# Products of values over the last 64 keys: from 64x64 pieces of the array to 128 rows padded with zeros

## The chip, the cores and the metric

The kernel runs on one core of a Trainium2 chip. A core has TensorE (PE in the profile, with its weight loads shown apart as PEld), VectorE (DVE), ScalarE (ACT), GpSimd (POOL) and SyncE (SP), which here only issues DMAs. The metric is the device time of one launch in microseconds (us); lower is better. Before the change the median of four runs is 1345.78 us (1345.26 to 1347.38).

## The reference, cut to what matters

Attention with a hard threshold is followed by a two-layer MLP with a squared ReLU. All of it is in fp32.

```
batch, n_heads, seq, head_dim = (8, 8, 576, 64)
scores = scale * np.matmul(q, k.transpose(0, 1, 3, 2))
thresh = np.max(scores, axis=-1, keepdims=True) - tau
scores = np.where(scores >= thresh, scores, -1000000000.0)
attn = np.exp(scores - np.max(scores, axis=-1, keepdims=True))
attn = attn / (np.sum(attn, axis=-1, keepdims=True) + 1e-09)
attn_out = np.matmul(attn, v)                 # the products of values
x = attn_out.transpose(0, 2, 1, 3).reshape(B * S, H * D)   # 4608 x 512
h = x @ w_in                                  # 512 x 2048
out = (np.maximum(h, 0.0) ** 2) @ w_out       # 2048 x 512
```

## The kernel before, in words

**Tiling.** Two heads of one batch make a pair, u = 0 and 1, and a pair is one visit `n`; there are 36 visits. The 576 queries and the 576 keys are each four blocks of 128 and a rest of 64. A step handles one block of 128 queries for both heads: `scores` or `scores_of_two` (TensorE), `maxima` (VectorE, L305), `exponents` (ScalarE, L317 to L320), `threshold` (VectorE, L332 to L335), `divide` (GpSimd, L340 and L342).

**Transposed weights.** The products of values contract over keys, so keys must lie on the partitions. `wT` holds the transposed attention weights: 128 partitions, ten groups of 64 queries, and nine columns of keys. Columns 0 to 3 are the four key blocks of head 0, columns 5 to 8 those of head 1, and column 4 (`NBLK`) is shared: the 64 last keys of one head lie on partitions 0 to 63 and those of the other on partitions 64 to 127. In the first 11 visits `turn` fills `wT` with TensorE transposes (L381, L388, L394) and ScalarE copies (L382, L390, L395). From visit 11 on (`by_dma`) `turn_blocks` transposes 32x32 blocks on VectorE into `turned` (L425 to L435), `set_aside` writes these to DRAM (`aside`, L403), and `place_blocks` brings them to their partitions by DMA (L443 and, for the rest of 64 queries, L452 and L460). All of these DMAs are issued in program order by SP.

**Products of values.** `mix(n, cols)` is the subject (L493 to L526). The stationary operand is a tile of values `vs`, keys by 64 columns, and the moving one is `wT`. Head 0 writes partitions 0 to 63 of a PSUM bank and head 1 partitions 64 to 127, so its matmuls use half the columns of the array each: "128\*64" in the profile. The last 64 keys have only 64 rows: "64\*64". In the first 11 visits `mix` runs once for every block of queries, 35 times in all: eight 128\*64 matmuls and two 64\*64 ones over 128 queries (over 64 for the rest block). Those calls are named early below. From visit 11 on it runs once a visit, 25 times, named late: group ONE is 320 queries (the region ONE or ODD of `wT` and the rest region LEFT), group TWO is 256 queries. It issues sixteen 128\*64 matmuls for both groups first and then four 64\*64 ones. For these, group ONE takes its heads' keys from (above, below) and group TWO from (below, above), so that the four products use four different quarters of the array. To make this possible `turn_blocks` swaps the two heads' rest keys for query blocks 2 and 3 (`i < 2` is the plain case): two narrow transposes instead of one. Each fp32 matmul shows as two records in the trace, a pair of heads as four.

**Values.** `load_v` loads `vs` (two buffers): the four key blocks of each head, and the last 64 keys of both heads into both halves of the partitions, since a head's keys are needed above for one group and below for the other.

**Order.** Each engine's instructions stand in the order in which the Python program records them; only semaphores tie engines together. A planner in the kernel spreads TensorE pieces of the MLP (`mlp_in` L544; `unit` L655; `mlp_out` L726; `product` L761) between the attention's steps, by constants of its own (`PIECE_US`, `VALUES_US`) that do not know the durations of `mix`. `put` copies `mix`'s results from PSUM to `xT` with ScalarE (L479, L483, L490). The functions that the change touches, and what calls them:

## Time and profile before

| | before |
|---|---|
| median of 4 runs | 1345.78 us |
| the profiled execution's own time | 1345.56 us |
| its span, first to last instruction | 1343.8 us |
| mean granted TensorE clock | 0.994 |
| busy: PE / DVE / POOL / ACT | 97% / 69% / 57% / 43% |
| `mix` (L496), PE busy | 169.9 us in 1700 records |
| ... of it 64\*64 records over 320, 256, 128 queries | 19.5, 16.7, 12.2 us |
| narrow transposes L429 and L430 (DVE) | 50 each, 202 and 204 ns |
| one transpose of both (L427, DVE) | 50, 270 ns |

The span is what the trace covers; the execution's own time has 1.8 us more around it. "Busy" counts the time in which at least one instruction of an engine runs, so that matmuls which run side by side in different parts of the array share it. An idle gap carries the name of what ended it: "[0.83 <-DVE w L332]" means 0.83 us idle until VectorE's instruction of line 332 had written `w`. A timeline row that merges several records shows the start of the first.

### The profile page before, as it was taken

What the parts mean: (1) busy time and instruction counts of PE and PEld (TensorE: products, weight loads), DVE (VectorE), ACT (ScalarE), POOL (GpSimd) and SP (SyncE); (2) the same over time, 40 slices, a digit from 0 to 9 for tenths busy, and PEclk for the clock granted to TensorE, in tenths of its full rate; (3) what the DMA queues carried; (4) which work ended last, traced back from release to release, by engine and by line L of the source; (5) the groups of instructions that cost most, each with busy time, mean ns of one, the idle gap of its engine ahead of it and who ended that gap; (6) DMA issues with size and microseconds to landing.
All of it is one profiled execution on the core that took longest, in us unless ns stands there. A gap on an engine that the chain in (4) does not pass through costs nothing.

```text
span 1343.8 us, 25020 instructions
## 1 busy us (share of the span) xinstructions
PE 1301.4 (97%) x9112; PEld 1078.8 (80%) x9112; DVE 924.9 (69%) x2026; ACT 581.7 (43%) x1357; POOL 761.5 (57%) x861
## 2 busy tenths in 40 slices
PE   6899999989999999999999999999999999999998
PEld 5676556878787878778897988888897888889997
DVE  6877775868687777777777776869687877632231
ACT  4777674225253434435353534343435353522421
POOL 3679775754654646474647463737374737354451
PEclk7999999999999999999999999999999999999999
DMA  7764531737696767766686766758686766430000
GB/s 155 164 160 113 145 91 35 163 84 189 147 215 137 191 163 172 167 154 159 147 201 156 179 175 133 177 137 192 139 199 156 177 166 149 136 92 1 17 17 16
DMA packets 331883, 187.04 MB, mean 139 GB/s; under 512 B 293200, under 2 KB 293232, under 8 KB 325360
## 3 DMA queue, kind: packets, MB, share of 16 engines
q1 hardware_dynamic: 326656, 176.22, 56.2%
q0 software_dynamic: 2800, 8.93, 1.9%
q8 instruction: 72, 1.18, 0.4%
q10 hardware_dynamic: 2304, 0.29, 0.2%
q14 instruction: 51, 0.42, 0.1%
HBM read 109.58 MB, written 68.42 MB: 132 GB/s over the span
## 4 chain that ended last, share of the span: by engine, by line
PE 84%; DVE 4%; ACT 4%; DMA 3%; SPq 1%; POOL 1%; issue 1%; DVEq 0%; POOLq 0%
PE big L761 28%; PE big L655 27%; PE big L496 11%; PE big L284 8%; PE big L544 3%; PE big L268 3%; PE big L726 2%; PE big L381 2%; DMA aside<-turned 1%; DVE w L332 1%; ACT w L320 1%; DVE st L305 1%; ACT wT L382 1%; DMA wT<-aside 1%; SPq L452 1%
## 5 line engine op out<-in xcount | busy, mean ns | idle before, releaser
L305 DVE TENSOR_REDUCE st<-big 128x1 f32<-128x576 f32 x288 | 204.7, 750 | 136.7 <-PE big L284 102.7
L342 POOL TENSOR_SCALAR w<-w,st 128x576 f32<-128x576 f32 x269 | 255.3, 958 | 27.8 <-DVE st L335 23.4
L340 POOL TENSOR_SCALAR st<-st 128x2 f32<-128x2 f32 (+1 forms) x148 | 35.6, 241 | 369.6 <-DVE w L332 364.9
L761 PE MATMUL big<-wo,gsum 128*128 128x256 f32 x1088 | 245.0, 382 | 0.0
L761 PEld LDWEIGHTS big<-wo,gsum 128*128 128x128 f32 x1088 | 204.3, 190 | 38.6 <-issue 11.7
L332 DVE SCALAR_TENSOR_TENSOR w<-big,st,w 128x576 f32<-128x576 f32 x269 | 206.9, 805 | 36.6 <-ACT w L320 36.1
L761 PE MATMUL big<-wo,g 128*128 128x256 f32 x816 | 186.4, 382 | 0.0
L655 PE MATMUL big<-xT,w_in_sb 128*128 128x128 f32 x1536 | 185.6, 276 | 0.0
L320 ACT ACTIVATE w<-big,st 128x576 f32<-128x576 f32 x269 | 183.5, 733 | 0.0
L655 PEld LDWEIGHTS big<-xT,w_in_sb 128*128 128x128 f32 x1536 | 179.0, 192 | 3.8 <-issue 3.1
L496 PE MATMUL big<-wT,vs 128*64 128x128 f32 (+7 forms) x1700 | 169.9, 358 | 11.5 <-ACT wT L382 4.0
L761 PEld LDWEIGHTS big<-wo,g 128*128 128x128 f32 x816 | 151.2, 190 | 26.3 <-issue 7.2
L496 PEld LDWEIGHTS big<-wT,vs 128*64 128x64 f32 (+1 forms) x1700 | 97.3, 137 | 80.3 <-issue 25.5
L317 ACT ACTIVATE st<-st 128x2 f32<-128x2 f32 (+1 forms) x148 | 30.1, 204 | 256.3 <-DVE st L305 255.5
L667 DVE TENSOR_TENSOR g<-big,g 128x512 f32<-128x512 f32 x96 | 65.2, 681 | 87.7 <-PE big L655 83.5
L284 PE MATMUL big<-kT,qT 64*128 64x256 f32 (+3 forms) x768 | 108.8, 416 | 4.8 <-ACT seen L297 2.7
L284 PEld LDWEIGHTS big<-kT,qT 64*128 64x128 f32 x768 | 85.1, 186 | 21.3 <-issue 5.6
L425 DVE STREAM_TRANSPOSE turned<-w 128x512 f32<-128x512 f32 x100 | 70.3, 703 | 25.6 <-DMA aside<-turned 22.8
L534 POOL TENSOR_TENSOR gsum<-g 128x512 f32<-128x512 f32 x34 | 45.1, 1326 | 74.0 <-ACT g L664 71.9
L663 ACT ACTIVATE g<-g 128x512 f32<-128x512 f32 x96 | 60.2, 627 | 57.4 <-DVE g L667 57.3
L664 ACT ACTIVATE g<-g 128x512 f32<-128x512 f32 x128 | 80.7, 630 | 4.1
L431 DVE STREAM_TRANSPOSE turned<-w 128x512 f32<-128x512 f32 x100 | 66.9, 669 | 0.0
(112 smaller groups left out, 1960.5 us busy)
## 6 DMA issues: line engine op xcount, KB each, us to landing
aside<-turned SPq DMA_DIRECT2D x50, 1152.0 KB, 4.5
wT<-aside SPq DMA_DIRECT2D x200, 288.0 KB, 5.3
vs<-in_v_dram SPq DMA_DIRECT2D x72, 128.0 KB, 5.6
ql<-in_q_dram SPq DMA_DIRECT2D x126, 72.0 KB, 4.5
wo<-in_moe_w_in_dram SPq DMA_DIRECT2D x16, 512.0 KB, 4.6
wo<-in_moe_w_out_dram SPq DMA_DIRECT2D x16, 512.0 KB, 3.6
out_dram<-osb POOLq DMA_DIRECT2D x32, 256.0 KB, 3.4
kl<-in_k_dram SPq DMA_DIRECT2D x113, 72.0 KB, 3.0
```

Source lines behind the costliest of these rows:

```text
L284: nc.tensor.matmul(big[to, at + x0:at + x1], lhsT, keys[u * D:(u + 1) * D, x0:x1], start=True, stop=True)
L305: nc.vector.tensor_reduce(out=mx[:, u:u + 1], in_=sc[u], axis=AX.XY, op=ALU.max)
L320: nc.scalar.activation(out=w[:, u, :].rearrange("p (h k) -> p h k", h=2), in_=sc[u], func=AF.Exp, bias=bias[:, u:u + 1], scale=SCALE)
L332: nc.vector.scalar_tensor_tensor(out=wu, in0=sc[u], scalar=thr[:, u:u + 1], in1=wu, op0=ALU.is_ge, op1=ALU.mult, accum_out=sm[:, u:u + 1])
L342: nc.gpsimd.tensor_scalar(out=w[:, u, :], in0=w[:, u, :], scalar1=z[:, u:u + 1], scalar2=rcp[:, u:u + 1], op0=ALU.add, op1=ALU.mult)
L425: move(wb[:, 0:h, :, :], whole_[:, 0, :, :, :])
L431: move(wb[:, h + 1:, :, :], whole_[:, 1, :, :, :])
L496: nc.tensor.matmul(ps[u * D:(u + 1) * D, :], vs[n % 2][rows, u * (NBLK + 1) + c, :], wT[rows, at // REST:(at + ps.shape[1]) // REST, NBLK ...
L655: nc.tensor.matmul(to[:, f, :], factor(j, p, q, c)[:, f * P:(f + 1) * P], part[:, c, :], start=(p in "125" and f == 0 and c == 0), stop=(p ...
L664: nc.scalar.activation(out=to, in_=to, func=AF.Square)
L667: nc.vector.tensor_tensor(out=x, in0=to, in1=x, op=ALU.add)
L761: nc.tensor.matmul(to, left[:, f, :], wo[:, slot, f, :], start=(f == 0), stop=(f == HF - 1))
```

## The change

The last 64 keys' values of head u now lie in rows `u * 64` to `u * 64 + 63` alone, and the other 64 rows of that tile are set to zero once, at the start, in both buffers (four memsets of 64x64 on GpSimd). Column 4 of `wT` keeps both heads' keys; a head's product now runs over all 128 rows, and the other head's weights meet zeros. All ten matmuls of a group are 128\*64, and a group's last keys follow its other blocks directly: first all of ONE, then all of TWO. The swap for query blocks 2 and 3 goes, and with it the split of one transpose in two. The values' last keys are loaded once, not twice: before visit 12 four DMAs a visit instead of six, later four of half the size for two of them.

```diff
+    def last_keys(t, u, filled=True):
+        half = u if filled else 1 - u
+        return t[half * D:(half + 1) * D, u * (NBLK + 1) + NBLK, :]
 def load_v(n):                                  # paired visits
-            for half in range(2):
-                loads.append((both[half * D:(half + 1) * D, :, NBLK, :], src[:, NBLK * P:S, :].rearrange("u p d -> p u d")))
+                loads.append((last_keys(t, u), src[u, NBLK * P:S, :]))
 ...                                             # the others
-            for half in range(2):
-                todo.append((t[half * D:(half + 1) * D, at + NBLK, :], v[b, h + u, NBLK * P:S, :]))
+            todo.append((last_keys(t, u), v[b, h + u, NBLK * P:S, :]))
 def turn_blocks(vis, i):
-            if i < 2:
-                move(wb[:, h, :, :].rearrange("p (u j) q -> p u j q", u=2), rest_[:, :, 0, :, :])
-            else:
-                move(wb[:, h, 2:4, :], rest_[:, 0, 0, :, :])
-                move(wb[:, h, 0:2, :], rest_[:, 1, 0, :, :])
+            move(wb[:, h, :, :].rearrange("p (u j) q -> p u j q", u=2), rest_[:, :, 0, :, :])
 def mix(n, cols):
-        groups = (one[:, 0:n1], at, (above, below)), (two[:, 0:n2], TWO, (below, above))
-        for ps, x, _ in groups:
-            for c in range(NBLK):
-                for u in range(2):
-                    term(ps, u, c, x, first=(c == 0))
-        for ps, x, places in groups:
-            for u, rows in enumerate(places):
-                term(ps, u, NBLK, x, rows, last=True)
+        def terms(ps, at):
+            for c in range(NBLK + 1):
+                for u in range(2):
+                    nc.tensor.matmul(ps[u * D:(u + 1) * D, :], vs[n % 2][:, u * (NBLK + 1) + c, :],
+                                     wT[:, at // REST:(at + ps.shape[1]) // REST, NBLK if c == NBLK else u * (NBLK + 1) + c, :],
+                                     start=(c == 0), stop=(c == NBLK))
+        terms(one[:, 0:2 * P + REST], at)
+        terms(two[:, 0:2 * P], TWO)
 ...                                             # at the start
+    for t in vs:
+        for u in range(2):
+            nc.gpsimd.memset(last_keys(t, u, False), 0.0)
```

## The prediction

> **What bounds the kernel now.** I read the page first, then the PE's busy time by stretch, then its idle gaps, and last the matmuls of `mix` one by one.

> ```profile
> PE 1301.4 (97%) x9112; PEld 1078.8 (80%) x9112; DVE 924.9 (69%) x2026; ACT 581.7 (43%) x1357; POOL 761.5 (57%) x861
> PE 84%; DVE 4%; ACT 4%; DMA 3%; SPq 1%; POOL 1%; issue 1%; DVEq 0%; POOLq 0%
> ```

> PE is busy for 97% and makes 84% of the chain of waits. Of the 42 us that PE is idle, almost all lies before 584 us; after that the waits view shows one gap of 0.3 us, and the last 3.5 us are the final stores. So late matmul time counts in full, and before 584 us I must look at each place.

> Now one late `mix`. Each row is the PE (or weight load) timeline asked at an instant, so its start is that of the oldest record still running.

> ```profile
> 809.04 0.75 PE L496 MATMUL big<-wT,vs 128*64 128x320 f32 x3
> 809.36 0.14 PEld L496 LDWEIGHTS big<-wT,vs 128*64 128x64 f32 x1
> 810.70 0.44 PE L496 MATMUL big<-wT,vs 128*64 128x320 f32 x2
> 812.32 0.60 PE L496 MATMUL big<-wT,vs 128*64 128x256 f32 x4
> 812.75 0.80 PE L496 MATMUL big<-wT,vs 128*64 128x256 f32 x6
> 813.07 0.76 PE L496 MATMUL big<-wT,vs 64*64 64x320 f32 x8
> 813.75 0.38 PE L655 MATMUL big<-held,w_in_sb 128*128 128x128 f32 x1
> ```

> Records of the two heads start together: the halves run side by side. The first pair of records takes 0.32 (809.04 to 809.36); the next take (810.70 - 809.36) / 5 = 0.268 over 320 queries, and (812.75 - 812.32) / 2 = 0.215 over 256. The last should end its slot at 812.97, but the first 64\*64 starts at 813.07: 0.10 for the change of shape. Then eight 64\*64 records, four at a time, hold PE until 813.75 (a slot of 0.32, one of 0.27, and 0.10 for the change back). Whole: 4.71 us.

> An early `mix` of 128 queries:

> ```profile
> 85.96 0.33 PE L496 MATMUL big<-wT,vs 128*64 128x128 f32 x2
> 86.78 0.54 PE L496 MATMUL big<-wT,vs 128*64 128x128 f32 x4
> 86.99 0.44 PE L496 MATMUL big<-wT,vs 64*64 64x128 f32 x4
> 87.35 0.33 PE L381 MATMUL big<-ident,w 128*128 128x128 f32 x1
> ```

> Eight pairs of records, the last at 86.78; a slot is 0.11, so 86.99 again holds 0.10 of change; the two 64\*64 products, which use two quarters only, take 86.99 to 87.35. Whole: 1.39 us.

> **Late: the four quarters go.** After, ONE and TWO have ten pairs of records each: 0.32 + 9 x 0.268 + 10 x 0.215 + 0.10 for leaving the shape = 4.98 against 4.71: +0.27 us a late `mix`. The 0.10 for 128\*64 to 128\*128 has no row; the same two shapes in the other direction (808.83 to 809.04 for a slot of 0.11), 128\*64 to 64\*64 and 64\*64 to 128\*128 all show 0.09 to 0.10, so I take 0.10. Its ends: nothing, or twice that. A row stands for each other term.

> [...]

> There are 25 late calls. Twenty-one lie where PE is continuous or on the chain that ends the gap behind them: 21 x 0.27 = +5.7. Four differ.

> *The call at 504.65.* The gap after it is ended by another chain (the stores and SP's DMAs since 493, which do not hold this `mix`):

> ```profile
> 528.76 1.51 PE L284 MATMUL big<-kT,qT 64*128 64x256 f32 x10 [0.83 <-DVE w L332]
> ```

> 0.83 swallows 0.27: I count 0 (ends 0 and +0.27).

> *The call at 277.9.* It is the first one, and what follows waits on SP:

> ```profile
> 283.10 11.27 SPq L452 DMA_DIRECT2D wT<-turned  x16
> 300.35 0.71 DVE L425 STREAM_TRANSPOSE turned<-w 128x512 f32<-128x512 f32 x1 [3.20 <-DMA aside<-turned]
> 303.41 2.20 PE L284 MATMUL big<-kT,qT 64*128 64x256 f32 x14 [0.51 <-DVE w L332]
> 306.85 0.70 PE L284 MATMUL big<-kT,qT 64*128 64x256 f32 x2 [1.23 <-ACT seen L297]
> ```

> SP has nothing to do from 280.65 to 283.10: its L452 overwrite the region LEFT, which in the old order is read last by the 64\*64 products at `mix`'s very end (283.07). In the new program these DMAs wait for ONE's last matmul, which ends before TWO's ten slots: 283.07 + 0.27 - 0.10 - 10 x 0.215 = 281.1, some 1.9 us earlier. Behind them on SP stand three loads and the store to `aside`, for whose landing VectorE waits 3.20 us; then come `threshold` and PE, with gaps of 0.51 and 1.23. ScalarE's exponents (done at 298.8) leave room. Up to 1.74 goes; the sum L667 of VectorE, which wants PE's L655 first, is late next and holds some of the 1.23. I take 1.3 off and 0.27 on: -1.0. Ends: +0.27 (nothing of it arrives) and -1.5. In the other visits the same early release only lets SP wait for a VectorE store later (L403), so no gain is counted.

> *The calls at 428.9 and 574.0.* Here PE waits inside `mix` for the DMA that brings TWO (gaps of 0.25 and 2.68). The new order puts two slots of 320 queries, 0.54, before that wait and takes 8 x 0.215 + 0.10 + 0.68 = 2.50 to 2.25, 0.25 less, after it. At 428.9 the gap of 0.25 goes and the end stays: 0. At 574.0:

> ```profile
> 276.19:279.60 3.41, 1.70 (x12) 1.46 (x14) 3.34 (x11) 0.00 (x0) 0.68 (x2) 1.00 0.85 136
> 576.56:579.97 3.41, 0.91 (x9) 0.77 (x11) 3.09 (x6) 1.66 (x4) 3.41 (x5) 1.00 1.05 133
> 579.97:583.38 3.41, 3.41 (x19) 1.44 (x16) 1.20 (x6) 0.15 (x1) 2.94 (x5) 0.50 0.36 55
> ```

> PE was busy for 0.91 of 3.41 us, and in the next 3.41 us the granted clock (the column after POOL) is 0.50; a stretch with 1.70 busy of 3.41 was followed by no such drop. After, the gap shrinks to 2.68 - 0.54 = 2.14, so at least 1.27 of 3.41 is busy: between the two rows, and either is possible. At half clock the remainder took 4.09; without it ten slots of 0.215 and 0.10 are 2.25. Ends: -0.3 (still slow) and -1.9; I take -1.0.

> [...]

> **Early: a change of shape goes.** With two products there were only two quarters in use, so a pair of heads over 128 rows costs the same slots. After: 0.82 + 2 x 0.11 + 0.21 = 1.25 against 1.39, -0.14 a call (a call over 64 queries comes out the same from its rows). Where `turn`'s L394 follows, itself 64\*64, the change of shape only moves: 7 calls at 0. Seven others lie in the first loop, where PE waits for VectorE 0.55 us a step and the chain passes them by, as it does five more between 98 and 209 us, where GpSimd's rounding or ScalarE holds it:

> ```profile
> 40.78 0.49 PE big L381 x3
> 41.30 0.86 ACT wT L382 x2
> ```

> Followed through all 35 calls, the chain of waits holds 16 whose saving counts: 16 x 0.14 = -2.2. Ends: -0.8 (other engines are close behind and take up two thirds) and -2.6.

> **The rest.** VectorE: 404 ns of two transposes become 270, 50 times; start to start it is 0.25 against 0.20, and only three pairs stand on the chain (at 301, 418 and 565 us): -0.15. Elsewhere PE's 97% hide it. The four memsets: POOL's next work after its start-up is at 15.49, after 11.4 us idle, and a 128x128 memset takes 0.22: nothing (with the cover gone at most 0.9). Values: 24 DMAs less on SP, at a median 0.53 each, in a stretch where SP is not on the chain: nothing, or -0.3. `put` of ONE runs under TWO now; ScalarE is not late behind `mix`: nothing. No wait is added.

> **Sum.** 5.7 + 0 - 1.0 + 0 - 1.0 - 2.2 - 0.15 = +1.3 us on the profiled 1345.56, which is 0.2 under the median of the runs. So 1347.1 for the median, with the price of leaving the shape, 37 times 0.10 either way, the widest of the unknowns.

> **Rivals.**
> - *Only the loss is real* (slower). The early saving is taken up by waits (-0.8), SP's early start does not reach PE (+0.27), the clock falls at 580 us again (-0.3), and 504.65 counts: 5.7 + 0.27 + 0.27 - 0.3 - 0.8 - 0.15 = +5.0, 1350.8. For it: ScalarE and VectorE end many early gaps of 0.24 to 1.4 us. Against it: between 66 and 90 and between 158 and 206 us the chain is nearly all PE. It counts as slower from +2.7, that is if 1.4 of the 4.3 us taken off above is missing. Chance 0.32.
> - *Leaving 128\*64 for 128\*128 is free* (faster). Then each of the 37 calls on the chain loses 0.10, and the slow first slot behind it (0.10 where 128-column weights follow): 1.3 - 37 x 0.2 = -6.1, 1339.7. It decides from 0.11 a call. Against it: every other change of shape, in the reverse direction too, shows 0.09 to 0.10. Chance 0.05.
> - *More waits shrink than I see* (faster): ScalarE and SP are released 2.2 us earlier in all 25 late calls, and the 9 us of gaps between 298 and 530 could lose 4 more: 1343. Against it: those gaps end on VectorE or ScalarE work that starts from scores. Chance 0.04.

> **How the numbers follow.** The forecast, gains and losses nearly cancelling, has 0.59. A measurement of this kernel can tell about 0.2%, 2.7 us, from no change: 1343.1 to 1348.5. The forecast's own range is 1345 to 1349.5, and some 0.09 of its 0.59 lies above 1348.5; of the first rival's 0.32 some 0.06, where half of the savings come, lies below. So same 0.59 - 0.09 + 0.06 + 0.01 of the third = 0.57, slower 0.35, faster 0.08. The range reaches to the first rival: 1344.0 to 1350.9.

> **What would show it.** No 64\*64 L496 rows; a late `mix` of 4.98 and an early one of 1.25 between the starts of its neighbours; SP's L452 near 281.3 in place of 283.1 and smaller gaps at 303 to 307; a gap of some 2.1 us inside the call near 574, with the clock behind it at 0.5 or 1. Wrong if the next matmul after `mix` starts directly at its slot's end, if early gaps grow by what `mix` saves, or if the clock falls at other places.

## The result and the profile after

The changed kernel takes 1348.12 us (median of 43 runs), the kernel before 1345.86 us (64 runs). The ratio is 1.0017 with a 95% interval of 1.0012 to 1.0022: 2.3 us slower, where 1.3 was forecast, and inside 0.2%. The profiled execution took 1347.66 us, its span is 1345.9 us.

The page after: busy time of the engines, and the chain of waits by engine.

```profile
PE 1304.4 (97%) x9112; PEld 1088.9 (81%) x9112; DVE 924.1 (69%) x1976; ACT 583.2 (43%) x1357; POOL 761.4 (57%) x865
PE 83%; DVE 5%; ACT 4%; DMA 3%; SPq 2%; POOL 1%; issue 1%; DVEq 0%; POOLq 0%
```

PE is busy 3.0 us longer and the bound is the same. Next, one late call of `mix` and one early call, PE asked at instants as before; `mix` is L497 now.

```profile
808.12 0.49 PE L497 MATMUL big<-wT,vs 128*64 128x320 f32 x2
812.59 0.60 PE L497 MATMUL big<-wT,vs 128*64 128x256 f32 x4
812.81 0.39 PE L497 MATMUL big<-wT,vs 128*64 128x256 f32 x2
813.12 0.38 PE L643 MATMUL big<-held,w_in_sb 128*128 128x128 f32 x1
```

```profile
85.66 0.33 PE L497 MATMUL big<-wT,vs 128*64 128x128 f32 x2
86.69 0.28 PE L497 MATMUL big<-wT,vs 128*64 128x128 f32 x2
86.90 0.33 PE L384 MATMUL big<-ident,w 128*128 128x128 f32 x1
```

The late call takes 813.12 - 808.12 = 5.00 us where it took 4.71; the early one 1.24 where it took 1.39. Leaving the shape costs what was assumed: 813.12 - 812.81 is a slot of 0.215 and 0.10.

The place near 277 us, now 2 us earlier: SP's stores of the rest region and PE's gaps behind them.

```profile
275.94 7.15 PE L497 MATMUL big<-wT,vs 128*64 128x320 f32 x40 [2.57 <-DVE w L335]
280.96 11.53 SPq L451 DMA_DIRECT2D wT<-turned  x16
298.46 0.71 DVE L428 STREAM_TRANSPOSE turned<-w 128x512 f32<-128x512 f32 x1 [0.91 <-DMA aside<-turned]
302.52 2.20 PE L287 MATMUL big<-kT,qT 64*128 64x256 f32 x14
305.32 0.70 PE L287 MATMUL big<-kT,qT 64*128 64x256 f32 x2 [0.60 <-ACT seen L300]
```

The call ends at 283.0, but SP starts at 280.96, with ONE's end: two of PE's gaps, 0.51 and 1.23 before, are 0 and 0.60. The call itself took 7.15 us, not 5.2. The windows view tells why (the clock is the column after POOL):

```profile
273.06:276.47 3.41, 0.84 (x5) 0.34 (x5) 2.80 (x6) 0.00 (x0) 0.00 (x0) 1.00 0.71 114
276.47:279.88 3.41, 3.41 (x15) 2.93 (x15) 3.34 (x9) 0.31 (x3) 2.66 (x3) 0.50 0.44 69
575.05:578.46 3.41, 1.92 (x16) 0.73 (x12) 3.41 (x8) 0.82 (x3) 3.41 (x4) 1.00 1.22 181
578.46:581.87 3.41, 3.27 (x24) 2.48 (x25) 2.44 (x7) 1.58 (x5) 2.94 (x4) 1.00 0.44 60
```

In this execution the clock fell to a half at 276.5 us and not near 580; in the profiled execution before it was the other way round. So the two profiles each carry one such window, at different places. And the gap inside the call near 574:

```profile
578.60 2.38 PE L497 MATMUL big<-wT,vs 128*64 128x256 f32 x20 [1.63 <-DMA wT<-aside]
```

Comparing the starts of the same call in the two traces (after minus before) gives the course: -0.14 us at the first call, -1.44 at the last early one (236.7), -1.97 at 277.9, -1.53 at 331.3, -0.67 at 428.9, -0.86 at 480.5, -0.58 at 504.6, -0.23 at 553.3, +0.05 at 574.0, -2.11 at 631.0, and then about +0.28 a call to +1.79 at the last one; PE's end is +2.07.

Two traces can be compared only so far. A second trace of the kernel before (the last run below) differs from the first by -0.97 us at the first call, -1.22 at 277.9, +0.55 at 331.3 and +0.30 at PE's end, with no change in the program.

### The profile page after: what moved, and what is told of

Read it like the earlier page. It is cut to its first block, busy times and chain, and to the rows that moved or that the text cites. A ratio compares the mean times of both kernels' runs of the same rounds, so it can differ in the third digit from the quotient of the medians.

```text
span 1345.9 us, 24944 instructions
## 1 busy us (share of the span) xinstructions
PE 1304.4 (97%) x9112; PEld 1088.9 (81%) x9112; DVE 924.1 (69%) x1976; ACT 583.2 (43%) x1357; POOL 761.4 (57%) x865
## 4 chain that ended last, share of the span: by engine, by line
PE 83%; DVE 5%; ACT 4%; DMA 3%; SPq 2%; POOL 1%; issue 1%; DVEq 0%; POOLq 0%
PE big L749 28%; PE big L643 26%; PE big L497 11%; PE big L287 8%; PE big L532 3%; PE big L271 3%; PE big L714 2%; PE big L384 2%; DVE w L335 1%; DMA aside<-turned 1%; SPq L451 1%; ACT w L323 1%; DVE st L308 1%; ACT wT L385 1%; SPq L459 1%
## 5 line engine op out<-in xcount | busy, mean ns | idle before, releaser
L497 PE MATMUL big<-wT,vs 128*64 128x128 f32 (+3 forms) x1700 | 172.1, 354 | 10.0 <-ACT wT L385 4.2
L497 PEld LDWEIGHTS big<-wT,vs 128*64 128x64 f32 x1700 | 107.8, 138 | 73.3 <-ACT wT L385 7.8
L655 DVE TENSOR_TENSOR g<-big,g 128x512 f32<-128x512 f32 x96 | 65.1, 681 | 91.4 <-PE big L643 86.7
```

The lines of the kernel that those rows point to most:

```text
L497: nc.tensor.matmul(ps[u * D:(u + 1) * D, :], vs[n % 2][:, u * (NBLK + 1) + c, :], wT[:, at // REST:(at + ps.shape[1]) // REST, NBLK if c = ...
L655: nc.vector.tensor_tensor(out=x, in0=to, in1=x, op=ALU.add)
```

## The experiments

"Before" in each ratio is the kernel before, run beside it on the same chip. All line numbers in a profile are those of the kernel at hand.

**The early calls alone, and the late ones alone.**

```diff
 # late only: on the changed kernel, early calls
+                    rows = slice(u * D, (u + 1) * D) if halves and c == NBLK else slice(0, P)
 # early only: on the kernel before, early calls and their values
-            for u, rows in enumerate((above, below)):
-                term(ps, u, NBLK, cols.start, rows, last=True)
+            for u in range(2):
+                term(ps, u, NBLK, cols.start, last=True)
```

> The changed kernel with the 35 early calls put back to two 64x64 products each. Theory (a saved 0.15 us an early call reaches the end where PE carries the chain): an early call takes 1.39 us again, the last early call starts 1.3 us later than in the changed kernel, and the time is 1.3 us above it, some 3.6 us (0.27%) above the kernel before. Rival (the early savings are swallowed by waits on ScalarE and VectorE): the calls are longer but the time is that of the changed kernel, 2.3 us (0.17%) above before.

> The kernel before with only the early calls (visits 0 to 10) changed to 128 rows with zeros; all late calls keep their four quarters. Theory: early calls 1.24 us in place of 1.39, 1.3 us less at the end, ratio to before 0.9990. Rival (swallowed early, or given back at the gap near 277 us): no difference, 1.0000.

Late only: 1.0023 (1.0011 to 1.0035), median 1348.62 us. The interval holds both expectations. Its profiled execution is its slowest run (1353.14 us): PE waits 2.11 us for VectorE before 757.9, and a half-clock window follows at 759.0. Early only: 1.0010 (1.0000 to 1.0020), which is against the theory: the saving does not come out. In its trace the saving is there at first (the last early call starts 1.42 us earlier than in the kernel before, the call at 277.9 1.66 earlier), and gone at the next call (331.3: +1.31). Between them lies a half-clock window at 276.0 us, so SP's stores start at 282.8 in spite of the earlier call; the sixteen of them then take 12.20 us (11.27 before), and the store behind them lands late. VectorE in that run:

```profile
301.66 0.71 DVE L431 STREAM_TRANSPOSE turned<-w 128x512 f32<-128x512 f32 x1 [4.43 <-DMA aside<-turned]
```

A wait of 4.43 us, 3.20 before and 0.91 in the changed kernel. That place swallowed the saving in this execution; whether it does so in most is not shown by one trace. The clock alone does not explain the loss: the runs with a mean granted clock of 0.992 take 1347.8 us (8 runs), those of the kernel before beside them 1347.6 (13).

**The order of the groups.** All products keep 128 rows, but ONE's and TWO's last keys come at the end of the call.

```diff
-        terms(one[:, 0:2 * P + REST], at)
-        terms(two[:, 0:2 * P], TWO)
+        for blocks_ in (range(NBLK), (NBLK,)):
+            terms(one[:, 0:2 * P + REST], at, blocks_)
+            terms(two[:, 0:2 * P], TWO, blocks_)
```

> The changed kernel, but the last keys of both groups come after all other blocks of both groups, as in the kernel before; all products stay 128 rows. PE has the same work (5.0 us a late call). Theory (part of the cost came back through the order): SP's stores of the rest region wait for the end of the call near 276 us again, so the gaps of 0.5 and 1.2 us near 305 us are back, and the gap inside the call near 574 us grows by 0.54 us; 1.5 us above the changed kernel, 1.0028 of before. Rival (the order is worth nothing): the time of the changed kernel, 1.0017.

Measured 1.0038 (1.0024 to 1.0051), median 1351.33 us: PE's work is that of the changed kernel and the time is some 2.8 us more (the difference of the two ratios, uncertain by about 1.9 us). SP and PE of this run:

```profile
283.31 11.54 SPq L451 DMA_DIRECT2D wT<-turned  x16
304.06 2.20 PE L287 MATMUL big<-kT,qT 64*128 64x256 f32 x14 [0.84 <-DVE w L335]
307.50 0.70 PE L287 MATMUL big<-kT,qT 64*128 64x256 f32 x2 [1.23 <-ACT seen L300]
```

SP waits for the end of the call again and both gaps are back. This run and the changed kernel's both had their half-clock window in this call (277.0 and 276.5 us), so they can be compared: from the start of this call to the next, at 331, the order costs 1.54 us (+1.98 against +0.44 beside the trace before).

**The quarters of the array.** On the kernel before, both groups take their last keys from the same halves, so that the 64\*64 products use two quarters, not four.

```diff
-        groups = (one[:, 0:n1], at, (above, below)), (two[:, 0:n2], TWO, (below, above))
+        groups = (one[:, 0:n1], at, (above, below)), (two[:, 0:n2], TWO, (above, below))
 # and in turn_blocks the one transpose of the changed kernel
```

> The kernel before without the swap of the rest keys, so that both groups' 64x64 products use the same two quarters of the array; VectorE has the one transpose of the changed kernel in place of two narrow ones. Theory (the four quarters run side by side, two do not): the last keys of a late call take 0.10 + 0.32 + 0.27 + 2 x 0.215 + 0.10 = 1.22 us in place of 0.79, +0.43 in 23 to 25 calls: 10 us, ratio 1.0075. Rival (64x64 products in one pair of quarters overlap as well, or VectorE's saving matters): within 0.1% of before.

Measured 1.0063 (1.0049 to 1.0078), 8.5 us. Its late call and the next matmul:

```profile
813.05 5.22 PE L492 MATMUL big<-wT,vs 128*64 128x320 f32 x40
818.20 1.05 PE L651 MATMUL big<-held,w_in_sb 128*128 128x128 f32 x7
```

5.15 us against 4.71 with four quarters and 5.00 with 128 rows: in this kernel 64-row products pay where four fill the array; two by two they are 0.15 us worse than padding with zeros. VectorE's narrow transposes, gone here too, show nowhere.

**128 rows only where ONE's end is awaited.** Quarters from visit 12 on, 128 rows in visits 0 to 11; and the same with early calls of two 64\*64 products again, which leaves only the call near 277.

```diff
+        if not paired(n):
+            for ps, x, _ in groups:
+                for c in range(NBLK + 1):
+                    for u in range(2):
+                        term(ps, u, c, x, first=(c == 0), last=(c == NBLK))
+            groups = ()
```

> The kernel before with 128 rows and zeros in visits 0 to 11, so the first late call (near 276 us) too, with ONE finished before TWO; the four quarters stay from visit 12 on. Theory (SP's stores behind that call start when ONE ends): against the run with early calls alone, L452's first store 1.5 to 2 us earlier, the gaps near 303 to 308 us smaller by 1.5, 1.5 us less in all: ratio to before about 0.9995 to 1.0. Rival (the gap only moves to ScalarE): the time of the run with early calls alone, 1.0010.

> As the kernel with 128 rows up to visit 11, but the 35 early calls are two 64x64 products each again: the only thing left of the change is the first late call, ONE finished before TWO. Theory A (the early calls' 1.3 us reach the end): 1.3 us above that kernel, ratio 0.9994. Theory B (they are lost before 300 us, and only the early end of ONE helped): the same time as that kernel, 0.9984.

To visit 11: 0.9984 (0.9973 to 0.9994), median 1342.98 us. Visit 11 only: 0.9986 (0.9976 to 0.9997), 1345.01 us beside a before of 1346.46. Both intervals lie below 1. SP and PE in the second:

```profile
280.92 11.34 SPq L458 DMA_DIRECT2D wT<-turned  x16
305.27 0.70 PE L290 MATMUL big<-kT,qT 64*128 64x256 f32 x2 [0.59 <-ACT seen L303]
```

So the new form of the one call near 277 gives about 2 us in the kernel before (0.4 to 3.2). The order and the padding come together in this run; that the order is what helps is shown by the run that undoes it, and the padding alone makes a late call longer (by 0.28 us in the changed kernel). How much of the gain is SP's early start itself is open: at a mean granted clock of 0.994 visit 11 only takes 1345.0 us (5 runs) and the kernel before 1345.3 (9), while runs at 0.992 or less fall from 17 of 30 to 1 of 11. Whether the shorter gaps behind the call are what keeps the clock up was not tested by itself. The early calls' share, the difference of the two ratios, is 0.0002 with an uncertainty of about 0.0015: not settled by this pair either.

**The clock.** PE was given work that nobody reads in its two longest late gaps, first into a PSUM bank that turned out to be awaited, then into one whose readers were long done.

```diff
+        if n == 11:
+            warm(two[:, 0:P], 14)        # first form; 14 transposes of the identity
+            warm(bank[next(x for x in oldest if x > 4 and x not in kept.values())][:, 0:P], 14)   # second form
+            if n == 19 and x == TWO:
+                warm(two[:, 0:P], 10)
```

> The kernel before with work for PE in its two longest late gaps, whose results nobody reads: 14 transposes of the identity ahead of the call near 277.9 us, and 10 between ONE and TWO of the call near 574 us. Theory (a window with PE mostly idle halves the clock in some executions, whatever the change): no clock of 0.5 near 277 or 580 us, 1.5 to 2.5 us less in the median, and a narrower spread: ratio 0.9985. Rival (the halved clock costs nothing, since other engines are awaited then): same median and spread, 1.0000 or above by the added work.

> The changed kernel with the same fill at the same two calls. Theory (late calls cost 0.28 us each and early ones give 1.4 back, and the difference of the two kernels is not made by the clock): 2 to 4 us above the filled kernel before (0.15 to 0.3%). Rival (the clock's falls decide it): the two filled kernels are equal within 1 us.

> 128 rows up to visit 11, quarters from visit 12, both gaps filled as above, and the start filled too: 28 transposes behind the scores of step 1 and 16 in step 2, so that PE stays busy from 11 to 21 us. Theory (the half clock from 13.4 to 27.0 us lies on the chain through L268, L381 and the first call): the first call starts 4 to 5 us earlier, and with 1.5 us each from the early calls and the fills the time is 6 to 8 us under before, ratio 0.995. Rival (at the start PE waits for VectorE and ScalarE anyway): the start gives less than 1 us, ratio 0.998.

These three had the first form: 1.0026 (1.0014 to 1.0038), 1.0050 (1.0035 to 1.0065) and 1.0036 (1.0025 to 1.0047), all slower. None tests a fill that lies in the gap, since this one waited for the VectorE instruction that ends the gap and then stood in front of `mix`; the clock fell there all the same (at 278.6, 276.7 and 282.3 us). The first two, 1349.28 and 1352.22 us, are 2.9 us apart, inside the 2 to 4 of the theory, but not free of the clock's falls as it wanted. PE in the filled kernel before:

```profile
279.76 3.25 PE L495 MATMUL big<-ident 128*128 128x128 f32 x14 [3.31 <-DVE w L332]
```

The start's fill in the third of them waited in the same way, for ScalarE, and its first call started 6 us later. The second form lies inside the gap, here on the kernel before:

```profile
274.64 1.69 PE L495 MATMUL big<-ident 128*128 128x128 f32 x14
277.63 5.17 PE L500 MATMUL big<-wT,vs 128*64 128x320 f32 x40 [1.30 <-DMA ql<-in_q_dram]
```

> The kernel before with the same two fills as in the filled run above, but the first one in a PSUM bank whose last reader was done 7 us earlier, so that the 14 transposes lie inside the gap near 275 us and not behind it. Theory (half-clock windows make the spread): mean granted clock 0.995 in nearly all runs, as in the runs of the kernel before that saw no late half-clock window (1343.9 us), ratio about 0.9985. Rival (the halved clock hides behind other waits): median and spread of the kernel before.

> 128 rows and zeros up to visit 11, quarters after, with both fills inside their gaps. Theory: the two gains add, about 1342 us (the runs of that kernel at clock 0.995), ratio 0.997 to 0.998 of before. Rival (with the first call's early end the halved clock there no longer reaches the path): as without the fill, 0.9984.

> The kernel before itself, for a second trace of it. Theory (phase of the clock's windows): same instructions, but a half-clock window at another place than 580 us, most likely near 277 us, and there the stores L452 of SP and the gaps near 303 us are 2 us later than in the first trace. Rival: the clock falls at the same place in each execution. Ratio 1.000.

The kernel before, filled: 0.9996 (0.9986 to 1.0006), no gain. Its trace has no fall near 277 or 580, as expected, but one at 308 us, and only 2 of its 11 runs have the mean clock of 0.995 that was expected of nearly all. None has 0.992 or less, where the kernel before has 17 of 30; but at 0.994 it takes 1346.5 us (7 runs) against 1345.3 (9), so that the fill seems to cost there what the clock gives. The kernel before once more: 1.0004 (0.9995 to 1.0013), and in its trace the clock fell at 580 again and at 306.7, not near 277. So the rival "always the same place" falls, and so does my "most likely near 277". The windows before and at that fall, in the kernel before run again:

```profile
303.27:306.68 3.41, 2.18 (x14) 1.34 (x12) 3.12 (x7) 2.76 (x8) 3.41 (x4) 1.00 1.05 263
306.68:310.09 3.41, 3.41 (x18) 3.41 (x18) 2.96 (x8) 1.13 (x3) 1.55 (x3) 0.50 1.21 306
```

128 rows up to visit 11 and both gaps filled: **0.9971 (0.9961 to 0.9981)**, 1343.11 us beside 1346.46, the fastest of all against its own neighbour, and its trace has no late half-clock window at all. (Nor has that of visit 11 only, without a fill.) Its fill leaves the gap near 277 at 1.28 us:

```profile
274.74 1.69 PE L501 MATMUL big<-ident 128*128 128x128 f32 x14
277.71 5.49 PE L506 MATMUL big<-wT,vs 128*64 128x320 f32 x40 [1.28 <-DMA ql<-in_q_dram]
```

All its 8 runs have a mean granted clock of 0.995 or 0.996, against 3 of 12 in the same kernel without the fill. Whether this gains time is not settled: the two ratios, 0.9971 and 0.9984, differ by 0.0013 with an uncertainty of about 0.0015, the medians are 1343.11 and 1342.98 us, and at 0.995 the filled kernel takes 1342.7 us (6 runs), the other 1342.0 (3). What differs from the filled kernel before is in the traces: there the gaps of 0.48 and 1.23 us near 303 to 307 remain, and the clock falls behind them; here one of 0.85 is left.

## Why the prediction was right

The time lies in the range and on the forecast's side, 1.0 us above it. In the two traces PE's end moves by +2.07, which is made of -0.14 ahead of the first call, -1.30 over the early calls, -0.53 up to the call at 277.9 (five traces with the early calls of before have -0.1 to -0.3 there), +0.44 from there to 331.3, +1.58 to 574.0, -2.16 from there to 631.0 and +4.18 over the rest. The late calls outside the two places are 1.58 + 4.18 = 5.8, as forecast (5.7). Of the two places one came out dearer than forecast and one cheaper, as the half-clock window lay in one of them in each trace: that the two deviations (+1.4 and -1.2) nearly cancel in this pair is luck, on which the 2.3 of the medians does not rest. Point by point:

- *Late calls.* 4.98 predicted, 5.00 measured, +0.28 in the length of a call that PE does not wait in, at full clock (over the 16 calls from 631 us on 4.2 of 4.5 us are left at the end). Leaving the shape costs 0.10: the rival that has it free falls.
- *The quarters.* That they, and no smaller thing, are what the change gives up: the run with two quarters loses 8.5 us, as worked out in the same way (10).
- *277.9.* -1.0 predicted, made of -1.3 for SP's early start and +0.27 for the call. SP's stores did start 2.1 us earlier and the two gaps fell from 1.74 to 0.60. In the pair of traces the place still costs +0.44, since the call itself ran at half clock. That the early start is worth the forecast 1.3 or so is shown by undoing the order (1.54 us, two traces with the fall in the same call); doing that call alone (0.9986) agrees, but how much of that gain goes with the clock is open.
- *The early calls* are the term that was mis-sized. A call saves 0.15, as predicted, but I counted 16 of them, -2.2. In the trace 12 calls arrive with 0.146 each, 1.75, and 0.45 is given back near 115 and 141 us, where PE's gaps end on VectorE (1.20 us before, 1.42 after) and on ScalarE (0.53 and 0.90): -1.30 from the first call to 236.7, so the term is 0.9 too large. Whether even that reaches the end stays open: in three comparisons it was not separable from nothing, and in one of them (early only) it was lost.
- *504.65.* "0.83 swallows 0.27: I count 0" rests on a reading that fails: the chain that ends the gap does hold this call. In the chain of the kernel before it stands ahead of PE's L284, and SP's L452 behind that:

```profile
504.72 4.72 PE big L496 x38
513.08 2.19 PE big L284 x14
515.27 0.12 SPq L452
```

From there to 553 the changed kernel's trace goes from -0.58 to -0.23, +0.35, and the gap near 528 is still there (0.95 us). But one trace does not settle what the call costs here: over the same stretch the traces of kernels that leave this call as it was move by -0.90 to +0.91 us, and those of the other kernels with longer calls here (0.28 or 0.43 us) by -0.30 to +0.45. The call at 428.9 came out 0.2 better than the 0 I counted, from there to 480.5, and is no firmer (+0.06 in late only).
- *574.0.* -1.0 was taken between -0.3 and -1.9; the trace has -2.16, since the gap shrank to 1.63 and the clock stayed up. Most of this is the clock: the same call took 9.07 us before and 6.85 after, but 7.46 and 6.98 in two runs that leave it unchanged (to visit 11, visit 11 only) and whose clock did not fall there. Of the gap's 1.05 us only 0.54 was forecast; the DMA came earlier too. That the 50% busy window keeps the clock and the 27% one does not was the right reading, but the sum treated the clock as a property of a place. It is one of an execution, as the last section shows.
- *Nothing* for memsets, DMAs, VectorE: not contradicted. VectorE's busy time fell by 0.8 us, and no gap was seen to move with it.
- *The first rival* (only the loss is real, +5.0) did not come, though its doubt about the early calls was right in part. *The third* (4 us more of the gaps between 298 and 530 go) did not come either: they fall from 8.96 to 7.44 us, all of it at 298 to 307 and at 431.6, where the forecast itself had counted 1.3 and 0.25.

## What to carry to other kernels

Padding a 64-row product with zeros to the full rows was dearer here than four 64x64 products that fill the array's quarters (5.00 us a late call against 4.71, +0.28 before rounding), cheaper than two at a time (5.15), and saved a change of shape where only two are to be had (an early call took 1.24 us against 1.39). Look, too, at what reads the operand last: finishing one group before the next starts let a DMA overwrite its region 2 us earlier, and in one call out of 25, where that DMA stood on the path, this was worth 1.5 to 2 us, five to seven times the price of the call. Where work that nobody reads (1.69 us of transposes) went into memory that nothing in the gap is waiting for, PE did it inside the gap near 275 us, and no half-clock window followed there in either trace; where it went into an awaited bank, it started only as the gap ended, after 3.31 us of waiting in the kernel before, and the clock fell there, at 278.6 us. No gain of time from filling a gap is shown.

## What the runs showed of the hardware that was not expected

**Most of the spread goes with the mean granted clock.** The kernel before, 75 runs beside the experiments, by mean granted clock of the run: 0.995: 1343.9 us (12 runs); 0.994: 1345.1 (19); 0.992: 1347.4 (38). The changed kernel: 0.995 and 0.996: 1346.7 (7 runs); 0.994: 1348.6 (12); 0.993: 1348.4 (22); 0.992: 1350.5 (3). The six other runs of the kernel before are five at 0.993, 1345.2 us, and one at 0.991. At the same clock the changed kernel is 2.8 to 3.5 us slower, more than the 2.3 of the medians, for only 3 of its 44 runs have 0.992. A window at half clock takes, by estimate, 3.41 / 2 = 1.7 us of PE's work (the call near 276 us took 7.15 us in the changed kernel, with such a window in it, and 5.50 in the same form in visit 11 only, without one), and in 1345 us it lowers the mean by 1.7 / 1345 = 0.0013; so the 3.5 us from 0.995 to 0.992 are, by estimate, two windows that count in full. The mean does not say where they lie: the two traces of the kernel before have the same 0.994, one with one late window and one with two but one fewer in the first 30 us. That it loses the clock less often fits its shorter gaps at 303 to 307 and 574; this link was not tested by itself.

**With transposes by the identity in the gap the clock stayed up in both traces.** In the two traces with the second form the 14 of them, 1.69 us, stand in the gap near 275 us, and no half-clock window follows there. With them PE is busy for 67% and 63% of the window of the grid that holds them, or most of them; without them it would be, by estimate, 18% and 21%, and every late window of 38% or less in the other traces was followed by half clock. So here they counted as work.
